# Fewer, larger loads in a delta-rule and gated-MLP kernel, and two kinds of transfer moved to ScalarE's queue

## The chip, the cores and the metric

The kernel runs on one core of a Trainium2 chip. A core has TensorE (PE: matrix products; its weight loads are listed as PEld), VectorE (DVE), ScalarE (ACT), GpSimd (POOL) and SyncE (SP, which only issues transfers and waits). The engines run side by side and meet at semaphores; each works through its own instructions strictly in order. Transfers (DMA) are carried by 16 DMA engines, whoever issues them. The metric is the device time of one execution in microseconds.

## The reference

The first half is a delta-rule attention, for each of 4 batches and 8 heads, with head size 48, over 768 steps in time. The second half is a gated MLP over its output.

```
k_n = k / (norm(k) + 1e-6)
for t in range(768):
    y[t]  = q[t] @ state                        # state: 48 x 48 for each head
    v_old = state^T @ k_n[t]
    state = state + beta[t] * outer(k_n[t], v[t] - v_old)

x = y, heads side by side                       # 4 x 768 x 384
h = relu(x @ w_in);  u, v = the two halves of h # 512 + 512 columns
v = (v - mean(v)) / sqrt(var(v) + 1e-6)
out = (u * (w_spatial @ v + b_spatial)) @ w_out # 4 x 768 x 384
```

All of it is float32. The MLP's products are made from two parts of each operand (`xh`, `xl`, `win_h`, `win_l` and so on), so that three products stand for one.

## The kernel before

**Chunks and steps.** The 768 time steps are cut into chunks of 64. One *step* of the kernel is one chunk of one batch with all eight heads (four pairs `u`, two halves `h` of the partitions): 48 steps, in two interleaved chains of two batches each. Within a chunk the recurrence becomes small matrix products with the inverse of a 64 x 64 triangular matrix per head.

**Groups and their inverses.** Four steps make a *group*; there are 12. For each step of a group `kk` loads K transposed (`k`, 112 partitions), multiplies it with itself on PE and masks and scales the result into `ta` on DVE (L595). When all four steps are there, `bounce` stores `ta` to DRAM (`ad`, two stores, L609) and `load_la` fetches the two 32 x 32 diagonal blocks of each matrix in another layout (`la`, four loads, L619): one block per partition, and each block twice, since two halves of the partitions work on the even and the odd columns of the same inverse. `lanes` copies a part of `la` into PSUM on ACT (L629, two copies), runs some 60 small substitution operations on DVE (L635 and L642), copies the result to `w` on ACT (L649), stores it to DRAM (`wd`, two stores, L655) and fetches it back into `ta` (four loads, L661). Group 0 goes another way (`lanes16`, `widen`) with 16 x 16 blocks.

**A step.** `load_kq` fetches K and Q transposed (`kq`, L680), `load_vk` fetches V and K in natural layout (`vk`, L684), each into one of three buffers; POOL scales V (L688). `step_t` transposes a part of the inverse (DVE, L703); `step_ef` completes the 64 x 64 inverse from its blocks (PE, with ACT's copies L717 and L729 between); `step_ab` takes the state's part off V (DVE L748) and multiplies with the inverse (DVE L764 writes `us`); `step_c` carries the state on (L792); `step_qk` and `step_d` make the output, which ACT writes to `xs` (L837). All small products of PE go through one helper, so they share line L412.

**The MLP.** When four chunks of a batch are done, `convert` packs them with six small transfers inside SBUF (L861), and ACT and POOL split `x` in its two parts (L868, L872). `mlp_v`, `mlp_u`, `mlp_g` and `mlp_o` (L903, L969, L1001, L1056) are the large products, which fill PE between the steps; ACT and DVE empty their PSUM tiles (among others L918, L980, L1018, L1037, L1065). The weights are loaded in pieces (`load_w`, L431 and L435) and split, mostly in the first third. L1239 are products with no use but to keep PE active.

**What sets the order.** The program is unrolled, and the order of the instructions on every engine is written by a planner in the kernel itself (`Line`). Every piece of work is a generator that yields an `Op`: its engine, how long it holds the engine (`occ`), when its result is there (`lat`), when it may begin (`dep`) and when it is due. The planner always takes the operation that can begin first by its own clock, and among those that are near, the one due first. What the operations really take on the chip is not known to it: an instruction whose input is late holds up everything behind it on its engine. A transfer costs SP 0.5 by this clock, and its data is taken to be there after `lat` (for a block load `la` 4.2):

```python
    return Op("SP", 0.5, lat, dep, due)
```

All transfers before are issued by SP. The bias, for comparison, is loaded in three pieces of one row that is repeated into two partitions (L1205):

```python
    out=x[32 * j : 32 * j + 2], in_=b_sp[j * 256 : j * 256 + 256].unsqueeze(0).broadcast_to([2, 256])
```

Of the kernel before, what the change touches and what calls it, by code (L numbers as in the profile page):

```python
# [7 lines left out]
F32 = mybir.dt.float32  # L8
# [11 lines left out]
G = 4  # L20
# [5 lines left out]
NG2 = NB * NT // 2  # L26
ND = DH // 128
KR = 112
EPS = 1e-6
LAG = 6  # L30
TG = 4
# [187 lines left out]
def dma(dep, due, lat=3.5, slack=0.0):  # L219
    if slack:  # L220
        first = dep

        def dep():
            t = first()
            return t if not t else t + slack

    return Op("SP", 0.5, lat, dep, due)


def now():  # L230
# [5 lines left out]
def delta_rule_gated_mlp(  # L236
    ctx: ExitStack,
    tc: tile.TileContext,
    kq_t: bass.AP,
    k_nat: bass.AP,  # L240
    vk_nat: bass.AP,
    b_nat: bass.AP,
    w_in: bass.AP,
    w_sp: bass.AP,
# [9 lines left out]
    def sb(name, *shape, dt=F32):  # L254
        return const.tile([128, *shape], dt, name=name)
# [72 lines left out]
    tmps = [sb(f"tmp{i}", 512) for i in range(2)]  # L328
    sms = [sb(f"sm{i}", 8) for i in range(4)]

    vks = [sb(f"vk{i}", 2 * NU * HD + 16) for i in range(3)]
    kqs = [const.tile([KR, 2, NU, CH], F32, name=f"kq{i}") for i in range(3)]
    kts = [const.tile([KR, NU, CH], F32, name=f"k{i}") for i in range(2)]
    aqs = [sb(f"aq{i}", NU, CH) for i in range(2)]
    mcs = [sb(f"mc{i}", NU, CH) for i in range(2)]
    tns = [sb(f"tn{i}", NU, 32) for i in range(2)]
# [45 lines left out]
    def on(t):  # L382
        return lambda: t

    def due(x):
        return lambda: x
# [7 lines left out]
    def rows_t(h):  # L394
        return slice(h * 64, h * 64 + 64)
# [27 lines left out]
        return Op("PE", 0, 1.3 * w, both(dep, slots[kind].ready), d, kind, make), held  # L423


    def load_w(buf, hi, lo, src, d):
        n = src.shape[1]
        st = buf[:, :n]
        if src.dtype == F32:
            t = yield dma(now, d, 6.0)  # L430
            nc.sync.dma_start(out=st, in_=src)  # L431
        else:
            raw = buf[:, 512 : 512 + 2 * n].bitcast(U32).rearrange("p (n two) -> p n two", two=2)
            t = yield dma(now, d, 6.0)
            nc.sync.dma_start(out=raw, in_=src.bitcast(U32).rearrange("p (n two) -> p n two", two=2))  # L435
            w0, w1 = raw[:, :, 0], raw[:, :, 1]
            e = buf[:, 256 : 256 + n].bitcast(U32)
            t1 = yield act(on(t), d, n)
            nc.scalar.activation(out=st, in_=w0, func=AF.Identity, scale=2.0**-52, bias=1.0)
            t = yield dve(on(t), d, n, 0.5)  # L440
            nc.vector.tensor_scalar(
                out=e, in0=w1, scalar1=20, scalar2=0x7FF, op0=ALU.logical_shift_right, op1=ALU.bitwise_and
            )
            t = yield dve(on(t), d, n, 0.5)
            nc.vector.tensor_scalar(out=e, in0=e, scalar1=896.0, scalar2=1150.0, op0=ALU.max, op1=ALU.min)
            t = yield dve(on(t), d, n, 0.5)
# [36 lines left out]
    def weights(par):  # L483
        buf = (*stage, ubs[3])[par]
        t = 0.0
        while jobs and (par < 2 or len(jobs) > n_late):
            hi, lo, src, kind = jobs.pop(0)
            t = yield from load_w(buf, hi, lo, src, due({"in": 3, "sp": 12, "out": 13}[kind]))
# [75 lines left out]
    def mask(t):  # L564
# [6 lines left out]
        )  # L571
        done["mc", t] = x

    def kk(t):
        g = t // G
        d = due(4 * g - 9)
        k = kts[t % 2] if t >= 2 * G else (
            xsb[t // 4][0:KR, t % 4 * 256 : t % 4 * 256 + 256].rearrange("p (u t) -> p u t", t=CH)
        )
        yield dma(at(("pk", t - 2) if t >= 2 * G + 2 else None), due(4 * g - 11), 3.5 if t < 2 * G else 6.0, 1.0)  # L580
        nc.sync.dma_start(out=k, in_=kq_t[t][:, 0])
        landed = line.t["SP"] + (3.0 if t < 2 * G else 5.5)
        free = [("b", s) for s in range((g - TG) * G, (g - TG) * G + G)] if g >= TG else []
        op, held = tiles_op(
            "anti",
            both(on(landed), at(("mc", t) if t >= G else None, *free)),
            d,
            lambda p: [mm(p[rows_t(h), u], k[rows_d(h), u, :], k[rows_d(h), u, :]) for u, h in UH],
            CH,
        )  # L590
# [4 lines left out]
        nc.vector.tensor_tensor(out=t_of(t), in0=psl(p[1], CH), in1=mcs[t % 2], op=ALU.mult)  # L595
        slots["anti"].give(p, x)
        done["kk", t] = x
# [5 lines left out]

    def bounce(g):
        d = due(4 * g - 7)
        ad = ad_g[g] = dram.tile([CH, 2, G * NU, CH], F32, name="ad")
        for h in range(2):
            t = yield dma(at(*(("kk", s) for s in range(g * G, g * G + G))), d, 4.5)
            nc.sync.dma_start(out=ad[:, h], in_=flat(g)[rows_t(h)])  # L609
        done["ad", g] = t  # L610

    def load_la(g):
        d = due(4 * g - 7)
        src = ad_g[g].rearrange("j h n t -> (h n) j t")
        for blk in range(2):
            for par in range(2):
                l0, r0 = par * 64 + blk * 32, blk * 32
                t = yield dma(at(("ad", g), ("lanes", g - 2) if g > 2 else None), d, 4.2)
                nc.sync.dma_start(out=las[g % 2][l0 : l0 + 32], in_=src[:, r0 : r0 + 32, r0 : r0 + 32])  # L619
        done["la", g] = t  # L620

    def lanes(g):
# [26 lines left out]
        nc.scalar.copy(out=ws, in_=w)  # L649
        done["wo", g] = t  # L650
        wd = dram.tile([32, 2, 2, G * NU, 32], F32, name="wd")
        wdl = wd.rearrange("c k h n t -> (k h n) c t")
        for par in range(2):
            t1 = yield dma(on(t), d, 4.5)
            nc.sync.dma_start(out=wdl[:, par::2, :], in_=ws[rows_t(par)])  # L655
        done["wd", g] = t1
        for blk in range(2):
            for h in range(2):
                r0 = h * 64 + blk * 32
                t = yield dma(on(t1), d, 4.0)  # L660
                nc.sync.dma_start(out=flat(g)[r0 : r0 + 32, :, blk * 32 : blk * 32 + 32], in_=wd[:, blk, h])  # L661
        done["T", g] = t


# [10 lines left out]
    def v_of(s):  # L675
        return vks[s % 3][:, 0 : NU * HD].rearrange("p (u e) -> p u e", e=HD)

    def load_kq(s):
        done["kq", s] = yield dma(at(*((n, s - 3) for n in ("qk", "d", "a") if s >= 3)), due(s - 2), 5.0, 1.0)
        nc.sync.dma_start(out=kqs[s % 3], in_=kq_t[s])  # L680

    def load_vk(s):
        t = yield dma(at(*((n, s - 3) for n in ("b", "c") if s >= 3)), due(s - 2.5), 5.0, 1.0)
        nc.sync.dma_start(out=vks[s % 3], in_=vk_nat[s])  # L684
        done["kn", s] = t
        v = v_of(s)
        x = yield pool(both(on(t), at(("cn", s // G))), due(s - 1.5), 192)
        nc.gpsimd.tensor_tensor(  # L688
            out=v, in0=v, in1=cns[s // G][:, s % G, 0].unsqueeze(2).broadcast_to([128, NU, HD]), op=ALU.mult
        )  # L690
        done["vs", s] = x
# [164 lines left out]
    def convert(j, xs, t):  # L856
        x = xs[1].rearrange("p (u t) -> p u t", t=256)
        for h in range(2):
            for i in range(NK):
                t1 = yield dma(on(t), lately(0.3), 2.4)  # L860
                nc.sync.dma_start(  # L861
                    out=x[h * 64 + 48 : h * 64 + 64, i],
                    in_=x[h * 64 + i * 16 : h * 64 + i * 16 + 16, 3],
                )
# [362 lines left out]
            line.spawn(lanes16())  # L1227

    def steps(s):
        for f in (load_kq, load_vk, step_t, step_ef, step_ab, step_c, step_qk, step_d):  # L1230
            line.spawn(f(s))
        if ORDER[s][2] == 0:
            line.spawn(zero(s))
# [104 lines left out]
```

## Time and profile before

| | |
|---|---|
| median of the runs | 597.86 us |
| the three runs | 594.10, 597.86, 601.64 us |
| the profiled execution | 594.68 us, its span 593.0 us |
| mean granted clock of TensorE | 0.902 |
| DMA, mean over the span | 64.31 MB, 108 GB/s |
| packets under 512 B, of all | 107,542 of 140,160 |

The span reaches from the first to the last instruction. Busy time is what an engine's own instructions cover; SP has none, and its issues are listed as SPq. The chain of waits starts from the last instruction and goes back, at each point, to what released it: its shares add up to the span, and they tell what ended last, which busy time doesn't. In a group's line the instructions are named by line, engine, operation and tiles (written<-read). A transfer's time to landing is counted from its issue to its semaphore.

Until 406 us, when the last inverses are loaded back (L661), steps, inverses and MLP share the engines; the last step's load is issued at 472 us (L680). What comes after is nearly all MLP.

### The profile page before, as it was taken

How to read it: one execution, taken by the hardware profiler on the slowest of the kernel's cores; microseconds unless marked ns; L12 is line 12 of the kernel's file. 1: busy time of each engine (PE TensorE's matmuls, PEld its weight loads, DVE VectorE, ACT ScalarE, POOL GpSimd, SP SyncE). 2: the span in 40 equal slices, each digit the busy share in tenths (PEclk: the TensorE clock that was granted, in tenths of full speed). 3: DMA queues.
4: the chain of work that ended last, by engine and by line, in shares of the span. 5: the costliest groups of instructions: out<-in, count | busy, mean ns of one | idle time of the engine just before them, and what ended most of it. 6: DMA issues, size and time to landing. Idle time of an engine off the chain costs nothing.

```text
span 593.0 us, 22265 instructions
## 1 busy us (share of the span) xinstructions
PE 521.4 (88%) x9404; PEld 474.3 (80%) x9404; DVE 352.9 (60%) x1436; ACT 216.8 (37%) x536; POOL 139.5 (24%) x210
## 2 busy tenths in 40 slices
PE   5935889889778997979999989999999999988997
PEld 5834868778657786979997878889988899977996
DVE  5799585977857988857995685871135422132220
ACT  3224334532334556223326456321256511155111
POOL 5452233652235242312204153120000000000000
PEclk9675586978878999979999899999999999997999
DMA  8767385676935766457736536333012200010001
GB/s 222 213 109 168 92 175 146 182 193 135 222 99 132 178 138 134 103 148 143 179 67 118 154 86 141 120 92 77 28 32 72 67 14 15 28 33 2 1 28 55
DMA packets 140160, 64.31 MB, mean 108 GB/s; under 512 B 107542, under 2 KB 130204, under 8 KB 140060
## 3 DMA queue, kind: packets, MB, share of 16 engines
q1 hardware_dynamic: 140060, 62.88, 43.7%
q8 instruction: 74, 1.21, 0.9%
q14 instruction: 26, 0.21, 0.1%
HBM read 47.55 MB, written 14.02 MB: 104 GB/s over the span
## 4 chain that ended last, share of the span: by engine, by line
PE 58%; DVE 18%; DMA 8%; SPq 6%; issue 5%; ACT 4%; POOL 1%; DVEq 0%; ACTq 0%; POOLq 0%
PE pt L412 21%; PE pm L1001 9%; PE pm L969 6%; PE pw L1001 6%; DVE prod L635 4%; DVE pw L642 4%; PE pm L1056 4%; PE pm L903 3%; PE pw L1056 3%; PE pw L903 2%; DMA kq<-in_kq_t 2%; PE pw L969 1%; SPq L861 1%; DVE ta L595 1%; SPq L619 1%
## 5 line engine op out<-in xcount | busy, mean ns | idle before, releaser
L642 DVE TENSOR_TENSOR pw<-pw,prod 128x30 f32<-128x30 f32 (+6 forms) x330 | 81.6, 251 | 5.4
L635 DVE TENSOR_TENSOR prod<-pw,la 128x30 f32<-128x30 f32 (+6 forms) x330 | 78.7, 241 | 6.9 <-ACT pw L629 1.7
L412 PE MATMUL pt<-kq,st 48*64 48x64 f32 x768 | 56.3, 239 | 2.1 <-ACT xs L837 1.7
L1001 PE MATMUL pm<-wsp_h,vh 128*128 128x256 f32 x192 | 57.4, 299 | 0.0
L412 PE MATMUL pt<-aq,us 64*64 64x64 f32 x768 | 54.4, 235 | 3.3 <-issue 3.0
L1001 PE MATMUL pm<-wsp_l,vh 128*128 128x256 f32 x192 | 54.7, 285 | 0.0
L1001 PE MATMUL pm<-wsp_h,vl 128*128 128x256 f32 x192 | 54.6, 284 | 0.0
L688 POOL TENSOR_TENSOR vk<-vk,cn 128x192 f32<-128x192 f32 x48 | 24.5, 512 | 116.7 <-DMA vk<-in_vk_nat 97.9
L412 PEld LDWEIGHTS pt<-aq,us 64*64 64x64 f32 x768 | 45.0, 149 | 3.5 <-issue 3.1
L412 PEld LDWEIGHTS pt<-kq,st 48*64 48x64 f32 x768 | 44.8, 148 | 3.6 <-ACT xs L837 1.8
L569 POOL TENSOR_TENSOR mc<-mpos,cn 128x256 f32<-128x256 f32 x46 | 28.9, 638 | 62.1 <-DVE cn L557 27.9
L412 PE MATMUL pt<-kq 48*64 48x64 f32 x768 | 37.9, 241 | 5.3 <-DMA kq<-in_kq_t 3.9
L412 PE MATMUL pt<-tn,ta 64*64 64x32 f32 x768 | 35.3, 237 | 7.3 <-DVE tn L703 3.8
L1239 PE MATMUL pm<-ones 128*128 128x256 f32 x216 | 39.5, 333 | 2.5 <-ACT ones L274 2.5
L1037 ACT CAST gh<-tmp 128x512 fp32r<-128x512 f32 x24 | 14.8, 619 | 70.3 <-DVE tmp L1018 70.2
L412 PE MATMUL pt<-us,vk 64*64 64x48 f32 x704 | 33.6, 235 | 7.5 <-DVE us L764 6.6
L412 PEld LDWEIGHTS pt<-tn,ta 64*64 64x64 f32 x768 | 30.8, 154 | 10.9 <-DVE tn L703 5.7
L412 PE MATMUL pt<-ta,pi 64*64 64x32 f32 x768 | 35.5, 235 | 3.8 <-ACT pi L717 2.0
L412 PE MATMUL pt<-k 48*64 48x64 f32 x640 | 30.4, 242 | 9.2 <-DMA k<-in_kq_t 6.8
L1001 PEld LDWEIGHTS pm<-wsp_h,vh 128*128 128x128 f32 x192 | 36.9, 192 | 1.5
L1018 DVE TENSOR_TENSOR tmp<-pm,ub 128x512 f32<-128x512 f32 x16 | 11.0, 688 | 45.4 <-PE pm L1004 45.4
L412 PEld LDWEIGHTS pt<-us,vk 64*64 64x64 f32 x704 | 28.1, 147 | 12.0 <-DVE us L764 8.8
(182 smaller groups left out, 1500.4 us busy)
## 6 DMA issues: line engine op xcount, KB each, us to landing
kq<-in_kq_t SPq DMA_DIRECT2D x48, 224.0 KB, 3.5
vk<-in_vk_nat SPq DMA_DIRECT2D x48, 200.0 KB, 3.4
ad<-ta SPq DMA_DIRECT2D x24, 256.0 KB, 4.2
la<-ad SPq DMA_DIRECT2D x44, 128.0 KB, 4.0
out<-ob SPq DMA_DIRECT2D x24, 192.0 KB, 1.9
k<-in_kq_t SPq DMA_DIRECT2D x40, 112.0 KB, 3.5
knn<-in_k_nat SPq DMA_DIRECT2D x10, 384.0 KB, 4.4
wd<-w SPq DMA_DIRECT2D x22, 128.0 KB, 3.6
```

What stands on the lines that cost most here:

```text
L412: return lambda: nc.tensor.matmul(*a, **dict(dict(start=True, stop=True), **k))
L569: (nc.vector if t in (0, 2) else nc.gpsimd).tensor_tensor(out=mc, in0=mall, in1=cns[t // G][:, t % G, 1].unsqueeze(2).broadcast_to([128, N ...
L635: nc.vector.tensor_tensor(out=pr, in0=w[:, :n, j : j + 1].broadcast_to([128, n, m]), in1=la[:, j, j + 1 : 32].unsqueeze(1).broadcast_to([1 ...
L642: nc.vector.tensor_add(out=w[:, :n, j + 1 : 32], in0=w[:, :n, j + 1 : 32], in1=pr)
L688: nc.gpsimd.tensor_tensor(out=v, in0=v, in1=cns[s // G][:, s % G, 0].unsqueeze(2).broadcast_to([128, NU, HD]), op=ALU.mult)
L903: nc.tensor.matmul(p[1], a[:, kt, ts], w[:, kt, DH:], start=(n == 0), stop=(n == 3 * NK - 1))
L969: nc.tensor.matmul(pu[:, k], w[:, kt, d0 : d0 + 128], a[:, kt], start=(n == 0), stop=(n == 3 * NK - 1))
L1001: nc.tensor.matmul(pg[:, k], v[:, d0 : d0 + 128], w[:, si, ts], start=(n == 0), stop=False)
L1018: nc.vector.tensor_tensor(out=gt, in0=pg, in1=ut[:, hs], op=ALU.mult)
L1037: nc.scalar.copy(out=gh[:, hs], in_=gt)
L1056: nc.tensor.matmul(p[1][:, :DM], a[:, dd, ts], w[:, dd], start=(n == 0), stop=(n == 3 * ND - 1))
L1239: nc.tensor.matmul(free[0].rearrange("p (n t) -> p n t", t=128), ones, ones.unsqueeze(1).broadcast_to([128, 2, 128]), start=True, stop=True,)
```

## The change

- **A step's loads.** `kq_t` and `vk_nat` become one input `kv_t`: for each step 128 rows of 912 numbers (K and Q transposed, then V and K natural, padded from 112 to 128 rows in the first part). `load_kq` and `load_vk` become `load_kv`, one load into one of three buffers, which waits for all readers of the buffer three steps back.
- **K of a group.** It comes by two steps with one load (all four steps of group 1 with one), from `kv_t`. From group 2 on there is one buffer of two steps instead of two buffers of one.
- **The bounce.** From group 1 on only the diagonal blocks are stored, by four stores (before: two stores of the whole matrices). They are then loaded by one load, whose source is repeated twice. The order of block and half in the lanes changes with it, in `wd` too.
- **Queues.** The six transfers that pack `x` and the two stores of the inverses are issued by ACT (`nc.scalar.dma_start`) instead of SP.
- **The planner.** A transfer costs SP 0.58 by its clock instead of 0.5, and ACT 0.6. Some latencies change (the block load 4.0 instead of 4.2, weights 4.5 instead of 6.0 with a slack of 1.5, K and step loads as in the diff); a K load's landing is now taken from the planned end of the load itself. A weight load becomes ready when its buffer's last piece is done, where before it was ready at once.

The core of the diff; the host's packing of `kv_t` is left out.

```diff
-    return Op("SP", 0.5, lat, dep, due)
+    return Op("SP", 0.58, lat, dep, due)
+
+
+def act_dma(dep, due, lat):
+    return Op("ACT", 0.6, lat, dep, due)
...
-    vks = [sb(f"vk{i}", 2 * NU * HD + 16) for i in range(3)]
-    kqs = [const.tile([KR, 2, NU, CH], F32, name=f"kq{i}") for i in range(3)]
-    kts = [const.tile([KR, NU, CH], F32, name=f"k{i}") for i in range(2)]
+    kvs = [sb(f"kv{i}", KV) for i in range(3)]
+    kqs = [x[0:KR, 0 : 2 * NU * CH].rearrange("p (a u t) -> p a u t", a=2, t=CH) for x in kvs]
+    vks = [x[:, 2 * NU * CH :] for x in kvs]
+    ktp = const.tile([KR, 2, NU, CH], F32, name="k")
...
-            t = yield dma(now, d, 6.0)
+            t = yield dma(on(t0), d, 4.5, 1.5)
...
-        k = kts[t % 2] if t >= 2 * G else (
-            xsb[t // 4][0:KR, t % 4 * 256 : t % 4 * 256 + 256].rearrange("p (u t) -> p u t", t=CH)
-        )
-        yield dma(at(("pk", t - 2) if t >= 2 * G + 2 else None), due(4 * g - 11), 3.5 if t < 2 * G else 6.0, 1.0)
-        nc.sync.dma_start(out=k, in_=kq_t[t][:, 0])
-        landed = line.t["SP"] + (3.0 if t < 2 * G else 5.5)
+        n = 2 if t < G or t >= 2 * G else G
+        if t % n == 0:
+            ks = ktp
+            if t < 2 * G:
+                ks = xsb[t // 4][0:KR, t % 4 * 256 : (t % 4 + n) * 256].rearrange("p (s u t) -> p s u t", s=n, t=CH)
+            kt_of[t // n, n] = ks
+            busy = [("pk", t - 1), ("pk", t - 2)] if t >= 2 * G + 2 else []
+            done["k", t] = yield dma(at(*busy), due(4 * g - 11), 4.0 if t < 2 * G else 5.0, 1.5)
+            nc.sync.dma_start(
+                out=ks.rearrange("p s u t -> p s (u t)"),
+                in_=kv_t[t : t + n, 0:KR, 0 : NU * CH].rearrange("s p c -> p s c"),
+            )
+        k = kt_of[t // n, n][:, t % n]
...
     def bounce(g):
         d = due(4 * g - 7)
+        if g:
+            ad = ad_g[g] = dram.tile([2, 2, G * NU, 32, 32], F32, name="ad")
+            for h in range(2):
+                for blk in range(2):
+                    r0, c0 = h * 64 + blk * 32, blk * 32
+                    t = yield dma(at(*(("kk", s) for s in range(g * G, g * G + G))), d, 4.0)
+                    nc.sync.dma_start(
+                        out=ad[h, blk].rearrange("n j t -> j n t"), in_=flat(g)[r0 : r0 + 32, :, c0 : c0 + 32]
+                    )
+            done["ad", g] = t
+            return
...
-        src = ad_g[g].rearrange("j h n t -> (h n) j t")
-        for blk in range(2):
-            for par in range(2):
-                l0, r0 = par * 64 + blk * 32, blk * 32
-                t = yield dma(at(("ad", g), ("lanes", g - 2) if g > 2 else None), d, 4.2)
-                nc.sync.dma_start(out=las[g % 2][l0 : l0 + 32], in_=src[:, r0 : r0 + 32, r0 : r0 + 32])
+        src = ad_g[g].rearrange("h k n j t -> (h k n) (j t)").unsqueeze(0).broadcast_to([2, 64, 1024])
+        t = yield dma(at(("ad", g), ("lanes", g - 2) if g > 2 else None), d, 4.0)
+        nc.sync.dma_start(out=las[g % 2].rearrange("p j t -> p (j t)"), in_=src)
...
-        wdl = wd.rearrange("c k h n t -> (k h n) c t")
+        wdl = wd.rearrange("c h k n t -> (h k n) c t")
         for par in range(2):
-            t1 = yield dma(on(t), d, 4.5)
-            nc.sync.dma_start(out=wdl[:, par::2, :], in_=ws[rows_t(par)])
+            t1 = yield act_dma(on(t), d, 4.5)
+            nc.scalar.dma_start(out=wdl[:, par::2, :], in_=ws[rows_t(par)])
...
-    def load_kq(s):
-        done["kq", s] = yield dma(at(*((n, s - 3) for n in ("qk", "d", "a") if s >= 3)), due(s - 2), 5.0, 1.0)
-        nc.sync.dma_start(out=kqs[s % 3], in_=kq_t[s])
-
-    def load_vk(s):
-        t = yield dma(at(*((n, s - 3) for n in ("b", "c") if s >= 3)), due(s - 2.5), 5.0, 1.0)
-        nc.sync.dma_start(out=vks[s % 3], in_=vk_nat[s])
-        done["kn", s] = t
+    def load_kv(s):
+        t = yield dma(
+            at(*((n, s - 3) for n in ("qk", "d", "a", "b", "c") if s >= 3)), due(s - 2.5), 4.5, 1.5
+        )
+        nc.sync.dma_start(out=kvs[s % 3], in_=kv_t[s])
+        done["kq", s] = done["kn", s] = t
...
-                t1 = yield dma(on(t), lately(0.3), 2.4)
-                nc.sync.dma_start(
+                t1 = yield act_dma(on(t), lately(0.3), 2.4)
+                nc.scalar.dma_start(
                     out=x[h * 64 + 48 : h * 64 + 64, i],
                     in_=x[h * 64 + i * 16 : h * 64 + i * 16 + 16, 3],
                 )
```

More of the change, by code (lines that the diff above doesn't have):

```diff
@@ L28 @@
 KR = 112
+KV = 2 * NU * CH + 2 * NU * HD + 16
 EPS = 1e-6
@@ L238, in delta_rule_gated_mlp @@
     tc: tile.TileContext,
-    kq_t: bass.AP,
+    kv_t: bass.AP,
     k_nat: bass.AP,
-    vk_nat: bass.AP,
     b_nat: bass.AP,
@@ L423, in tiles_op, with load_w @@
         return Op("PE", 0, 1.3 * w, both(dep, slots[kind].ready), d, kind, make), held
-    def load_w(buf, hi, lo, src, d):
+    def load_w(buf, hi, lo, src, d, t0):
         n = src.shape[1]
@@ L433, in load_w @@
             raw = buf[:, 512 : 512 + 2 * n].bitcast(U32).rearrange("p (n two) -> p n two", two=2)
-            t = yield dma(now, d, 6.0)
+            t = yield dma(on(t0), d, 4.5, 1.5)
             nc.sync.dma_start(out=raw, in_=src.bitcast(U32).rearrange("p (n two) -> p n two", two=2))
@@ L487, in weights @@
             hi, lo, src, kind = jobs.pop(0)
-            t = yield from load_w(buf, hi, lo, src, due({"in": 3, "sp": 12, "out": 13}[kind]))
+            t = yield from load_w(buf, hi, lo, src, due({"in": 3, "sp": 12, "out": 13}[kind]), t)
             left[kind] -= 1
@@ L572, in mask @@
         done["mc", t] = x
+    kt_of = {}
     def kk(t):
@@ L585, in kk @@
             "anti",
-            both(on(landed), at(("mc", t) if t >= G else None, *free)),
+            at(("k", t - t % n), ("mc", t) if t >= G else None, *free),
             d,
@@ L660, in lanes @@
                 t = yield dma(on(t1), d, 4.0)
-                nc.sync.dma_start(out=flat(g)[r0 : r0 + 32, :, blk * 32 : blk * 32 + 32], in_=wd[:, blk, h])
+                nc.sync.dma_start(out=flat(g)[r0 : r0 + 32, :, blk * 32 : blk * 32 + 32], in_=wd[:, h, blk])
         done["T", g] = t
@@ L1229, in steps @@
     def steps(s):
-        for f in (load_kq, load_vk, step_t, step_ef, step_ab, step_c, step_qk, step_d):
+        for f in (load_kv, step_t, step_ef, step_ab, step_c, step_qk, step_d):
             line.spawn(f(s))
@@ L1302 @@
     qt = dfirst(q)
-    kq_t = np.ascontiguousarray(np.stack([dfirst(k), qt], axis=2))
-    vk_nat = np.zeros((NST, 128, 2 * NU * HD + 16), k.dtype)
-    vk_nat[:, :, : NU * HD] = tfirst(v).reshape(NST, 128, NU * HD)
-    vk_nat[:, :, NU * HD : 2 * NU * HD] = np.roll(tfirst(k).reshape(NST, 128, NU * HD), 64, axis=1)
+    kv_t = np.zeros((NST, 128, KV), k.dtype)
+    kv_t[:, :KR, : NU * CH] = dfirst(k).reshape(NST, KR, NU * CH)
+    kv_t[:, :KR, NU * CH : 2 * NU * CH] = qt.reshape(NST, KR, NU * CH)
+    c0 = 2 * NU * CH
+    kv_t[:, :, c0 : c0 + NU * HD] = tfirst(v).reshape(NST, 128, NU * HD)
+    kv_t[:, :, c0 + NU * HD : c0 + 2 * NU * HD] = np.roll(tfirst(k).reshape(NST, 128, NU * HD), 64, axis=1)
     bt = beta.reshape(NB, NU, 2, NC_, CH).transpose(2, 4, 0, 3, 1).reshape(128, NST, NU)[:, perm_s]
@@ L1314 @@
     args_np = {
-        "kq_t": kq_t,
+        "kv_t": kv_t,
         "k_nat": tfirst(k),
-        "vk_nat": vk_nat,
         "b_nat": np.ascontiguousarray(bt),
```

## The prediction

> **What bounds the kernel now.** I read the page's busy shares first, then its chain of waits, the groups and sources of the issuing queue, and last the timeline where one load was late.
>
> ```profile
> PE 521.4 (88%) x9404; PEld 474.3 (80%) x9404; DVE 352.9 (60%) x1436; ACT 216.8 (37%) x536; POOL 139.5 (24%) x210
> PE 58%; DVE 18%; DMA 8%; SPq 6%; issue 5%; ACT 4%; POOL 1%; DVEq 0%; ACTq 0%; POOLq 0%
> PE pt L412 21%; PE pm L1001 9%; PE pm L969 6%; PE pw L1001 6%; DVE prod L635 4%; DVE pw L642 4%; PE pm L1056 4%; PE pm L903 3%; PE pw L1056 3%; PE pw L903 2%; DMA kq<-in_kq_t 2%; PE pw L969 1%; SPq L861 1%; DVE ta L595 1%; SPq L619 1%
> ```
>
> PE is busy for 88% of the span but holds only 58% of the chain; DVE's substitution in lanes (L635, L642) is next. What this change touches is the queue and the transfers: SPq 6% of 593.0 us is 36 us, DMA 8% is 47 us. No engine can gain more than that from them together, and only their removable part. The view of the sources gives the price of one issue (min/median/max in ns), and the view of transfers the time to landing (last column, us):
>
> ```profile
> L619 SPq DMA_DIRECT2D la<-ad x44: 303/564/2144, 29.0 to 368.2; - x44
> L609 SPq DMA_DIRECT2D ad<-ta x24: 466/492/761, 14.7 to 361.2; - x24
> L655 SPq DMA_DIRECT2D wd<-w x22: 597/660/1779, 75.6 to 400.4; - x22
> L861 SPq DMA_DIRECT2D xs<-xs x72: 512/586/1807, 88.1 to 533.4; - x72
> L581 SPq DMA_DIRECT2D k<-in_kq_t x40: 328/508/1639, 6.1 to 352.8; - x40
> L680 SPq DMA_DIRECT2D kq<-in_kq_t x48: 312/380/1723, 8.4 to 471.9; - x48
> ```
>
> ```profile
> kq<-in_kq_t SPq DMA_DIRECT2D x48, 224.0 KB, 3.5
> vk<-in_vk_nat SPq DMA_DIRECT2D x48, 200.0 KB, 3.4
> ad<-ta SPq DMA_DIRECT2D x24, 256.0 KB, 4.2
> la<-ad SPq DMA_DIRECT2D x44, 128.0 KB, 4.0
> knn<-in_k_nat SPq DMA_DIRECT2D x10, 384.0 KB, 4.4
> ta<-wd SPq DMA_DIRECT2D x44, 64.0 KB, 3.0
> xs<-xs SPq DMA_DIRECT2D x72, 16.0 KB, 1.8
> ub<-in_b_sp SPq DMA_DIRECT2D x3, 2.0 KB
> ```
>
> The last view is the one that sets my price for a late load: the chain, PE and ACT (idle time in brackets) around 156 us, where a kq load was late.
>
> ```profile
> 156.35 4.60 DMA kq<-in_kq_t
> ```
>
> ```profile
> 160.99 0.34 PE L412 MATMUL pt<-st,kq 48*64 48x48 f32 x1 [3.29 <-DMA kq<-in_kq_t]
> ```
>
> ```profile
> 162.21 0.27 ACT L729 COPY ta<-pt 128x128 f32<-128x128 f32 x1 [5.30 <-PE pt L412]
> 163.73 0.58 ACT L629 COPY pw<-la 64x512 f32<-64x512 f32 x1 [0.32 <-DMA la<-ad]
> 236.31 1.21 ACT L629 COPY pw<-la 64x512 f32<-64x512 f32 x2
> ```
>
> Of 4.60 us of lateness PE stood 3.29 us, a share of 0.72; ACT behind it stood 5.30. The order on every engine is fixed in advance, so whatever waits stops all that is queued behind it.
>
> **The change, part by part.** The sum is made against the profiled execution, 594.68 us with its span of 593.0; the median of the three runs shown, 597.86, is 3.2 higher, and they spread over 7.5.
>
> *One load per step.* kq and vk (48 + 48 issues) become 48 issues of 128 x 3,648 B, 456 KB. 48 x 0.380 = 18 us of SP issues go. Landing: knn's 384 KB takes 4.4 us, so some 5 against 3.5. It must wait for all five readers of step s-3; the kq load waits for the last of them (step_d) already, so v's scaling on POOL moves later by at most its wait for kq. Behind that load in SP's order are the K loads and the inverses, behind v's scaling L748 on DVE and the b product on PE. Ends: all of kq's 2% of the chain gone (-12 us) to 48 x 1.5 us later landing x 0.72 (+52). The load has step s-2 to land in, so I take -6.
>
> *K by two steps.* 48 issues become 23: 25 x 0.508 = 13 us of SP. From group 2 on there is one buffer of two steps, so a group's second pair waits for the first pair's products, and may come one landing later. Nine to ten such places x 4.4 us x 0.72 give at most +32; the products are due nine steps ahead of their group, which hides it: 0.
>
> *x and the inverses on ACT's queue.* 72 x 0.586 + 22 x 0.660 = 57 us of issues leave SP (SPq L861 has 1% of the chain, 6 us) and enter ACT's order. During 6 x 0.586 = 3.5 us per x tile ACT begins no copy of pi, ta or xs for the step in hand. If none is hidden that is 57 x 0.72 = +41; if all is, 0. ACT is at 37% and holds 4% of the chain, and the planner charges 0.6 each, so it can put urgent copies first: I take +5. SP's gain from this and from the four la issues that become one (33 x 0.564 = 19 us, SPq L619 another 1%) is 12 us, the two shares on the chain; ends -36 (all of SPq) to 0.
>
> *The bounce.* Two stores of 256 KB with 4 KB rows become four of 64 KB with 128 B rows in each group from 1 on: 22 more issues x 0.492 = 11 us of SP. The nearest row is ta<-wd, the same size and rows: 3.0 us, so 1.5 + 3.0 from the first issue against 0.5 + 4.2. That comes out even: 0, ends -2 to +1 us for each of 11 groups.
>
> *The group's blocks by one load.* This decides. Its destination is 128 rows of 4 KB, 512 KB; its source is written as a repeat of two in front of 64 rows (unsqueeze, broadcast to [2, 64, 1024]). Every large load of before has an outermost loop of 32 to 128 rows on both sides. The one transfer of the same form is the bias (L1205, a row repeated to [2, 256]): two packets of 1 KB, and the only row above without a landing time. It cannot tell whether a larger one is dealt by its 128 rows or by its repeat of two, so I bound it. The views of the transfers in two stretches (queue: packets, MB, share of 16 engines), and the busy share and GB/s of the first:
>
> ```profile
> q1 hardware_dynamic: 1245, 1.03, 89.3%
> ```
>
> ```profile
> 4.00:8.00 4.00, 4.00 (x140) 3.81 (x139) 3.01 (x8) 0.30 (x2) 3.58 (x12) 1.00 0.89 259
> ```
>
> ```profile
> q1 hardware_dynamic: 864, 1.18, 6.1%
> ```
>
> From 4 to 8 us (loads of 1 to 3 KB rows) one engine moved 1.03 MB / (16 x 4 x 0.893) = 18.0 GB/s; from 540 to 593 us (mostly output rows of 1.5 KB) 1.18 MB / (16 x 53 x 0.061) = 22.8 GB/s. Dealt over sixteen, 524 KB at 259 GB/s take 2.0 us, and with the 1.8 us that a 16 KB transfer takes to land, 3.8. Dealt over two, 262 KB each take 11.5 us (22.8) to 14.6 us (18.0), landing after 13.3 to 16.4. I take two engines, by the bias row, which alone has this form, and 13.3, since 4 KB rows are nearer to the longer ones.
>
> The Trainium skill, "DMA: Bandwidth & Descriptors", section "Why a DMA increments its semaphore by 16 and not by 1", states that a transfer is split along the outermost dimension that isn't 1, over the largest number of engines up to 16 that divides that dimension on both sides; its "Rules for kernel authors" name a leading repeat of c copies as confined to c engines. By that rule it would be two here, and at its 27 GiB/s per engine some 9 us of moving (an estimate from that page). No run here shows a broadcast load of this size yet; the bias row doesn't contradict it.
>
> Who waits: ACT's copy of la into PSUM (L629) stands in ACT's fixed order where the planner thinks that the load lands. Before, it began 6.3 us after the first la issue in group 5 and 9.3 in group 7:
>
> ```profile
> 157.43 3.60 SPq L619 DMA_DIRECT2D la<-ad  x4
> 227.03 3.29 SPq L619 DMA_DIRECT2D la<-ad  x4
> ```
>
> The planner charged three issues of 0.5 and 4.2, 5.7 us; it now charges 4.0, so the copy moves up by 1.7, to 4.6 and 7.6 after the issue, in the middle 6.1. ACT then stands 13.3 - 6.1 = 7.2 us, with pi, ta, xs and every MLP eviction behind it; DVE stands at the first L635 that reads that PSUM; and all of SP's later loads, the steps' among them, queue behind the blocks on those two engines. At 0.72 that is 5.2 us, and for 11 groups +57. Ends: none (sixteen engines) to 11 x (16.4 - 4.6) = +130.
>
> Sum: 594.7 - 6 - 12 + 5 + 57 = 639 for an execution like the profiled one; one like the median would be 3 higher. I take 640.
>
> **The rivals.** *Dealt over all sixteen (faster).* The load lands after 3.8 us, the planner's 4.0 is right, and three issues a group are saved: 594.7 - 13 = 582, or 571 if all of kq's share on the chain and another 5 us of SPq go. For it: 128 rows on the destination, as in every load that lands in 3 to 5 us. Against it: the source's form. The turning point is the landing: up to 6.1 us the copy doesn't wait, from about 7.5 us on (11 x 1.4 x 0.72 = 11) the saving is spent. *Late but covered (same).* The blocks do come after 13 us, but ACT's copy has fallen behind SP by then: the page of sources shows that copy waiting for its load in only three places, 1.6 us in all.
>
> ```profile
>   DMA la<-ad: 1.6, 3
> ```
>
> If the lead is 9 to 10 us, 11 x 3.5 x 0.72 = 28, or 18 with half of that under PE's MLP work: 594.7 - 13 + 18 = 600. Against it: with fewer issues SP is no later than before, and the copy's due time was moved up. *ACT's queue becomes the wait (slower by another way).* Blocks over sixteen, but the 94 issues on ACT cost their +41: 594.7 - 18 + 41 = 618. Against it: 4% of the chain. That an edit does nothing at all is excluded: the counts of issues are in the code.
>
> **How the numbers follow.** Forecast (two engines, the copy waits) 0.68; sixteen engines 0.16; late but covered 0.12; ACT's issues 0.04. The forecast's own range is 610 (594.7 - 13 + 28: cover of PE's MLP work halves the 57) to 690 (594.7 - 13 + 11 x 7.2 = 79, every microsecond passed on, a third as much again for the loads behind the blocks, and 3 for the median), and holds nine in ten of its 0.68. With the covered case, ACT's and the upper third of the faster case the range is 582 to 690. Two per cent, 12 us, is about what a measurement of this kernel can tell from no change. Faster by over 2% is the sixteen-engine case, 0.16; within 2% the covered one with the forecast's lowest edge, 0.14; slower 0.70.
>
> **What would show it.** Right: the block load's time to landing is 11 us or more (it may have no landing time, like the bias), ACT L629 heads the list of waits with about 7 us in each of 11 places, PE's idle time rises at those places, and SPq L861 is gone from the chain. If ACT L629 waits for nothing and the load lands in 4 us, the sixteen-engine rival holds. If L629 is prompt and ACT's L717 or L729 stand behind issues, it is ACT's queue. If PE waits for kv at many steps without a block load in front, the price of the merged load was mine to get wrong.

## The result and the profile after

The changed kernel takes 685.74 us (median of 4 runs, 677.30 to 685.81) against 599.25 us for the kernel before (median of 4 runs beside it): a ratio of 1.142, 95% interval 1.130 to 1.154. It is slower, as forecast, but the slowdown of 86 us is twice the forecast one of 42. The profiled execution took 685.81 us with a span of 684.1. Here and below, some executions of a kernel run at a lower granted clock and come out over 1.5% longer than its fastest: the ratios leave these out and compare the means of the others, while the medians count all executions, so that the two can differ by about 1%.

The page's busy shares, and below them its chain of waits. The chain's shares add up to only about half of the span: on the way back from the end it was lost, so they tell of the later half.

```profile
PE 543.0 (79%) x9500; PEld 496.1 (73%) x9500; DVE 357.1 (52%) x1436; ACT 217.4 (32%) x536; POOL 139.4 (20%) x210
PE 29%; DMA 9%; DVE 5%; ACT 3%; issue 2%; ACTq 2%; SPq 1%; DVEq 0%
PE pt L417 7%; PE pm L1021 6%; DMA la<-ad 4%; PE pw L1021 3%; PE pm L1076 3%; PE pw L1076 2%; PE pm L989 2%; DMA out<-ob 2%; PE pm L923 2%; ACTq L881 1%; PE pw L923 1%; DVE pw L664 1%; DVE prod L657 1%; DMA ta<-wd 1%; DMA ad<-ta 1%
```

No engine has more to do: DVE is at 357.1 us of work against 352.9, ACT at 217.4 against 216.8. PE's 22 us more come with a lower granted clock (0.837 over the span against 0.902). What grew most is idle time: 141 us of the span on PE, against 72 before. The block load la<-ad, which had no share worth a line before, now heads the transfers of the chain, and with it stand the output's store, the inverses' return (ta<-wd) and the blocks' stores. The view of the waits (us in total, times, longest) says who stands for them:

```profile
ACT pw L651 <- DMA la<-ad: 64.8, 8, 10.6
DVE prod L657 <- ACT pw L651: 30.7, 6, 7.7
ACT ob L1085 <- DMA out<-ob: 26.2, 7, 10.7
PE pt L417 <- DMA k<-in_kv_t: 19.4, 1, 19.4
PE pt L417 <- DMA kv<-in_kv_t: 10.8, 4, 3.9
```

ACT's copy of the blocks (L651, before L629) waits in 8 of the 11 groups for 8.1 us each; before it was 1.6 us in all. That is the wait that the prediction named. The third and fourth rows are of another kind: an output store and a K load have nothing to do with the blocks, and they are waited for longer than before (17.1 us and 6.8 us there). One place shows how they come together, in the timelines of SP and ACT:

```profile
388.92 0.55 SPq L641 DMA_DIRECT2D la<-ad  x1
389.57 14.04 SPq L1088 DMA_DIRECT2D out<-ob  x2
```

```profile
391.27 0.83 ACT L888 CAST xh<-xs 128x768 fp32r<-128x768 f32 x1 [0.59 <-PE pm L923]
402.75 0.48 ACT L1085 COPY ob<-pm 128x384 f32<-128x384 f32 x1 [10.65 <-DMA out<-ob]
```

SP issues the block load at 388.92 and right behind it, at 389.57, the store of a finished output tile. Stores of this kind landed after 1.9 us before; this one frees its buffer only 13 us later, and ACT stands 10.65 us for it. The chain and the windows of the stretch (busy time of PE, PEld, DVE, ACT, POOL, then the granted clock, the share of the 16 DMA engines and GB/s) show what happened in between:

```profile
389.57 13.16 DMA out<-ob
461.68 13.99 DMA la<-ad
```

```profile
395.00:400.00 5.00, 0.00 (x0) 0.00 (x0) 0.00 (x0) 0.00 (x0) 0.00 (x0) 0.66 0.13 52
```

For five microseconds no engine of the core does anything. The DMA engines are busy to a share of 0.13, which is 2 of 16, and move 52 GB/s, 26 each. This row is the direct sight of the two engines. It fits the 13.16 us of the output store that every other transfer behind the blocks has its own share on these two as well, and isn't complete until they have got to it. That holds for ACT's queue too: its two stores of the inverses were issued at 389.24 and 390.07 us, and of the packets moved from 395 to 400 us 62 are SP's (0.25 MB, the blocks) and 62 ACT's (0.01 MB); from 400 to 402 us it is 28 of each. Equal counts of such unequal packets say that the two queues took turns on the busy engines, one short row of the stores for one 4 KB row of the blocks.

The stop has an after-effect: the granted clock is 1.00 until 395 us, 0.66 in the row above, 0.50 from 400 to 405 and 0.55 to 407, and then 1.00 again. So the products right behind a stop run slower, which is a part of PE's 22 us more; how large a part was not summed up.

### The profile page after: what moved, and what is told of

Its sections match the earlier page's. It is cut to its first block, busy times and chain, and to the rows that moved or that the text cites. A ratio compares the mean times of both kernels' runs of the same rounds, so it can differ in the third digit from the quotient of the medians.

```text
span 684.1 us, 22247 instructions
## 1 busy us (share of the span) xinstructions
PE 543.0 (79%) x9500; PEld 496.1 (73%) x9500; DVE 357.1 (52%) x1436; ACT 217.4 (32%) x536; POOL 139.4 (20%) x210
## 4 chain that ended last, share of the span: by engine, by line
PE 29%; DMA 9%; DVE 5%; ACT 3%; issue 2%; ACTq 2%; SPq 1%; DVEq 0%
PE pt L417 7%; PE pm L1021 6%; DMA la<-ad 4%; PE pw L1021 3%; PE pm L1076 3%; PE pw L1076 2%; PE pm L989 2%; DMA out<-ob 2%; PE pm L923 2%; ACTq L881 1%; PE pw L923 1%; DVE pw L664 1%; DVE prod L657 1%; DMA ta<-wd 1%; DMA ad<-ta 1%
## 5 line engine op out<-in xcount | busy, mean ns | idle before, releaser
L657 DVE TENSOR_TENSOR prod<-pw,la 128x96 f32<-128x96 f32 (+10 forms) x330 | 77.9, 241 | 35.3 <-ACT pw L651 30.7
L664 DVE TENSOR_TENSOR pw<-pw,prod 128x96 f32<-128x96 f32 (+11 forms) x330 | 80.7, 250 | 4.4
L417 PE MATMUL pt<-kv,st 48*64 48x64 f32 x768 | 63.6, 256 | 0.9 <-DVE us L784 0.6
L417 PEld LDWEIGHTS pt<-ta,pi 64*64 64x64 f32 x768 | 36.5, 174 | 24.2 <-ACT pi L737 22.1
L417 PE MATMUL pt<-kv,ta 64*64 64x48 f32 x768 | 41.1, 252 | 16.2 <-ACT ub L1000 8.1
L417 PEld LDWEIGHTS pt<-kv,st 48*64 48x64 f32 x768 | 50.2, 165 | 3.2 <-issue 1.4
L417 PE MATMUL pt<-kv 48*64 48x64 f32 x768 | 39.3, 248 | 14.9 <-DMA kv<-in_kv_t 10.8
L417 PEld LDWEIGHTS pt<-kv,ta 64*64 64x64 f32 x768 | 35.0, 163 | 21.5 <-ACT ub L1000 8.3
L1259 PEld LDWEIGHTS pm<-ones 128*128 128x128 f32 x213 | 37.3, 252 | 14.8 <-ACT ob L1085 9.8
L417 PEld LDWEIGHTS pt<-kv 48*64 48x64 f32 x768 | 32.2, 156 | 17.9 <-DMA kv<-in_kv_t 8.4
```

The source lines that it names most:

```text
L417: return lambda: nc.tensor.matmul(*a, **dict(dict(start=True, stop=True), **k))
L657: nc.vector.tensor_tensor(out=pr, in0=w[:, :n, j : j + 1].broadcast_to([128, n, m]), in1=la[:, j, j + 1 : 32].unsqueeze(1).broadcast_to([1 ...
L664: nc.vector.tensor_add(out=w[:, :n, j + 1 : 32], in0=w[:, :n, j + 1 : 32], in1=pr)
L1259: nc.tensor.matmul(free[0].rearrange("p (n t) -> p n t", t=128), ones, ones.unsqueeze(1).broadcast_to([128, 2, 128]), start=True, stop=True,)
```

## The experiments

Ratios are to the kernel before, run on the same chip beside each kernel, with their 95% interval; medians are in us. Chips differ by up to 6 us in the kernel before (593 to 599), so ratios are what is compared.

**The repeat taken away.** The block load becomes two loads of 64 rows.

```diff
-        src = ad_g[g].rearrange("h k n j t -> (h k n) (j t)").unsqueeze(0).broadcast_to([2, 64, 1024])
-        t = yield dma(at(("ad", g), ("lanes", g - 2) if g > 2 else None), d, 4.0)
-        nc.sync.dma_start(out=las[g % 2].rearrange("p j t -> p (j t)"), in_=src)
+        src = ad_g[g].rearrange("h k n j t -> (h k n) (j t)")
+        for par in range(2):
+            t = yield dma(at(("ad", g), ("lanes", g - 2) if g > 2 else None), d, 4.0)
+            nc.sync.dma_start(out=las[g % 2][rows_t(par)].rearrange("p j t -> p (j t)"), in_=src)
```

> The changed kernel, with the one block load of a group issued as two loads of 64 rows without the repeat, 256 KB each, so that each has an outermost loop of 64 on both sides. Theory A (the repeat confines the load to two engines, and what waits for it makes the whole slowdown): the loads land after 3 to 5 us instead of 14, ACT's copy waits under 5 us in all instead of 64.8, and the time falls to 575 to 595 us. Rival B (the issues on ACT's queue, and SP's wait for the stores made there): the block load is only a bystander, the time stays above 640. Rival C (the merged step load is the wait): also above 640, with PE's waits for kv unchanged.

Measured: 604.91, ratio 1.011 (1.005 to 1.018). The source view of the copy, with the rows of its waits:

```profile
L652 ACT COPY pw<-la x22: 576/584/586, 38.5 to 390.5; 64x512 f32<-64x512 f32 x22
  issue: 1.6, 1
  DMA la<-ad: 0.7, 1
```

The copy's wait fell from 64.8 to 0.7 us and 0.13 of the 0.142 went with it. The loads land after 6.3 us (median), later than the 3 to 5 expected, and the time lies above what theory A expected: 10 us by the median, 6 if the ratio is taken on the 594 us of the kernel before. The blocks are nearly the whole slowdown, but what is left isn't faster than before either.

**The planner told of the slow load.** One number, `d, 4.0` to `d, 14.0`, in the changed kernel's block load.

> The changed kernel with one number changed: the planner is told that the block load takes 14.0 instead of 4.0. The load itself stays as it is, on two engines. Theory A1 (most of the cost is that ACT's copy stands in the order ten microseconds too early): the copy waits under 15 us in all, and the time falls by about 11 x 5 = 55 us, to 610 to 640. Theory A2 (most of the cost is that every later load queues behind the blocks on those two engines, and that the inverses come ten microseconds later): under 20 us are won, the time stays at 665 to 690.

Measured: 645.49, ratio 1.091 (1.081 to 1.102), between the two theories: by the ratios 0.051 of the kernel before is won, some 30 us, and 0.091, some 54 us, is still lost. In its source view the copy waits for nothing any more, but PE and ACT wait for other transfers (view of the waits):

```profile
PE pt L417 <- DMA kv<-in_kv_t: 23.4, 5, 7.3
PE pt L417 <- DMA k<-in_kv_t: 22.2, 3, 19.6
ACT ob L1085 <- DMA out<-ob: 22.0, 8, 6.2
POOL kv L708 <- DMA kv<-in_kv_t: 126.1, 21, 29.9
```

**The blocks' part alone on the kernel before.** The four stores, the repeated load, and the order of `wd` that goes with them; `load_kq`, `load_vk`, K, queues and the other numbers as before.

> The kernel before with the blocks' part of the change alone: four stores of the diagonal blocks and the one repeated load (planner's latency 4.0), all on SP, step loads, K loads, queues and the other planner costs as before. Theory A: it has nearly the whole slowdown, 660 to 690 us. Rivals B and C: without their parts it stays under 620.

Measured: 674.83, ratio 1.141 (1.132 to 1.150): the whole slowdown comes with this part.

**The queues put back.** The kernel with two block loads, and

```diff
-            t1 = yield act_dma(on(t), d, 4.5)
-            nc.scalar.dma_start(out=wdl[:, par::2, :], in_=ws[rows_t(par)])
+            t1 = yield dma(on(t), d, 4.5)
+            nc.sync.dma_start(out=wdl[:, par::2, :], in_=ws[rows_t(par)])
```

and the same for the packing of x.

> As the run with two loads of 64 rows, and the packing of x and the stores of the inverses put back to SP's queue. Theory A: the queues matter little, within 2% (12 us) of the run with two loads. Rival B: faster than that run by more than 12 us, and SP's wait for the stores of the inverses (37.7 us in the changed kernel) goes.

Measured: 595.16, ratio 1.004 (0.999 to 1.009). By the medians that is 10 us under the run with ACT's queue, by the ratios 4, and their intervals overlap; either way it is within the 12 us of theory A. The block loads land after 4.2 us here, against 6.3 there. SP's wait for the stores of the inverses is mostly gone, as rival B expected; in the run with ACT's queue and in this one:

```profile
SPq L684 <- DMA wd<-w: 31.9, 11, 5.9
```

```profile
SPq L684 <- DMA wd<-w: 8.7, 5, 3.5
```

With the stores on ACT, SP arrives at their return trip before they have landed in 11 places instead of 5, and everything behind it in SP's order waits. What this costs in time isn't clear of the noise.

**Two loads, and the planner told 14.0 all the same** (both `d, 4.0` to `d, 14.0`).

> The run with two block loads (604.9 us), with the planner told that each takes 14.0 although it takes some 4: the inverses come as late in the fixed order as in the run where the planner was told of the slow load (645.5 us), but no engine is held by the blocks. If the 40 us between those two runs come from the inverses standing ten microseconds later in the order, this run takes 635 to 650 us. If they come from the later loads that queue behind the blocks on two engines, it takes 600 to 615 us.

Measured: 617.72, ratio 1.036 (1.026 to 1.045), nearer to the second expectation and just outside it. Against the run with two loads in their early place (1.011) the late place costs 0.025 here; against the run told 14.0 (1.091), where the load holds two engines, 0.055 is won, some 33 us. The order isn't quite the same in these runs, since two loads are one issue more for each group.

**The blocks' part alone, with two loads.** The third experiment with the edit of the first.

> The kernel before with the blocks' part alone (as the run with 674.8 us), the block load issued as two loads of 64 rows without the repeat. Theory A: the whole of that run's slowdown goes, 585 to 600 us. If the four stores with 128 B rows were to blame for a part of it: 610 us or more. It also shows what this part would have been worth without the repeat: with 22 issues less for the loads and 22 more for the stores I expect no difference to the kernel before beyond 1%.

Measured: 587.19, ratio 0.988 (0.982 to 0.993). The four stores with their short rows cost nothing that shows; without the repeat this part alone gains a little more than 1%, where I had expected no more than that. Its transfers (KB each, us to landing):

```profile
la<-ad SPq DMA_DIRECT2D x22, 256.0 KB, 3.9
ad<-ta SPq DMA_DIRECT2D x44, 64.0 KB, 2.8
```

**The queues alone, and the merged step load alone, on the kernel before.** The first is the edit of the diff in `lanes` and `convert` with `act_dma`; the second has `kv_t`, `load_kv` and its three buffers, with K still loaded step by step, from `kv_t`.

> The kernel before with the packing of x and the stores of the inverses on ACT's queue (planner's cost 0.6 on ACT), nothing else changed. The difference between the two runs with two block loads (604.9 with ACT's queue, 595.2 without) says 600 to 608 us, 1 to 2% slower than before. If ACT's queue only hurts beside the merged loads and K pairs: 590 to 597 us.

> The kernel before with the step's two loads merged to one, K loads, blocks, queues and the other planner costs as before. The prediction put this part at -6 us: 585 to 590 us. If the issues it saves were not what ended last, within 1% of the kernel before; if the later landing counts, 600 us or more.

Measured: 593.49, ratio 0.989 (0.982 to 0.996) for the queues, the second branch: alone, ACT's queue doesn't hurt. That it hurts beside the other parts isn't shown, since 1.011 and 1.004 there have intervals that overlap. 591.08, ratio 0.990 (0.982 to 0.998) for the merged load: the median is just above the first range, and by the ratio it is 6 us under the kernel before, which is what the prediction gave it, with an interval of 1 to 11 us.

**The slow load issued by ACT.** In the run told 14.0:

```diff
-        t = yield dma(at(("ad", g), ("lanes", g - 2) if g > 2 else None), d, 14.0)
-        nc.sync.dma_start(out=las[g % 2].rearrange("p j t -> p (j t)"), in_=src)
+        t = yield act_dma(at(("ad", g), ("lanes", g - 2) if g > 2 else None), d, 14.0)
+        nc.scalar.dma_start(out=las[g % 2].rearrange("p j t -> p (j t)"), in_=src)
```

> The run where the planner was told 14.0 (645.5 us), with the repeated block load issued from ACT's queue instead of SP's; it still moves on two engines. If the 28 us between the late run with two loads (617.7) and that run come from SP's later loads standing in one line behind the blocks, they now stand in another line and most of it goes: 615 to 630 us. If they come from the two engines being busy, whoever asks, it stays at 638 to 655 us; ACT's wait for the stores of the blocks may add some.

Measured: 647.06, ratio 1.090 (1.084 to 1.097), the same as from SP. The queue that asks doesn't matter to the time, but it does to the waits: PE's for the steps' loads fall from 23.4 us to 5.8, those for K from 22.2 to 17.5, ACT's for the output's store from 22.0 to 15.6. Other idle time takes their place; whether it is ACT's own wait for the blocks' stores was not separated.

**Three parts together, and two parts alone.** The blocks with two loads, the merged load and ACT's queue, with K and the planner's numbers as before; then K by two steps alone (`kt_of`, one buffer of two); then the planner's numbers alone (`Op("SP", 0.58, ...)`, and `load_w` with `on(t0)`, 4.5 and 1.5).

> The kernel before with the merged step load, ACT's queue for x and the inverses, and the blocks' part with two loads of 64 rows, but with K step by step and the planner's other numbers as before. Each of the three alone measured 0.988 to 0.990 of the kernel before. If they add up: 0.965 to 0.975, about 577 us. If each only shortens the same line of SP: 0.985 to 0.995.

> The kernel before with K of a group by two steps (one buffer of two) alone. The run with two block loads and all the rest of the change stands at 1.011, though three of its parts alone are at 0.99. If the K pairs give that back: 1.01 to 1.03. The prediction put them at 0: 0.99 to 1.005.

> The kernel before with the planner's other numbers of the change alone: SP 0.58 for a transfer, weights 4.5 with a slack of 1.5 and ready only when the buffer's last piece is done. If the new order of the instructions gives the gain back: 1.01 to 1.03; if not, 0.99 to 1.005, and the K pairs remain.

Measured: 596.10, ratio 1.004 (0.999 to 1.008) for the three together, though each alone is at 0.988 to 0.990, above both expectations; 593.04, ratio 0.998 (0.994 to 1.002) for the K pairs, 0 as predicted; 584.59, ratio 0.987 (0.982 to 0.991) for the numbers alone, under both expectations, a gain where I had asked for a loss.

**The bytes alone.** The changed kernel, and the run told 14.0, with the same order of all instructions and a block load of a sixteenth:

```diff
+    for x in las:
+        nc.vector.memset(x.rearrange("p j t -> p (j t)"), 0.0)
...
-        src = ad_g[g].rearrange("h k n j t -> (h k n) (j t)").unsqueeze(0).broadcast_to([2, 64, 1024])
+        src = ad_g[g].rearrange("h k n j t -> (h k n) (j t)")[:, 0:64].unsqueeze(0).broadcast_to([2, 64, 64])
...
-        nc.sync.dma_start(out=las[g % 2].rearrange("p j t -> p (j t)"), in_=src)
+        nc.sync.dma_start(out=las[g % 2].rearrange("p j t -> p (j t)")[:, 0:64], in_=src)
```

> The changed kernel with the block load cut to the first two of each block's 32 rows (64 of 1,024 numbers per partition, 256 B; the rest of the buffer is zero, so most of the substitution works on zeros and the output isn't the reference's). Form, queue, count and the order of every instruction stay those of the changed kernel; only the bytes on the two engines fall to a sixteenth, and the landing to about 3 us. If the load's duration is the whole of what the blocks cost, as much is won as by two loads (604.9 us): 595 to 610. If the form costs something besides its duration, 620 or more.

> The same cut load in the run where the planner was told 14.0 (645.5 us): again the same order, with a load of about 3 us. If the 28 us that the slow load costs there beyond the late order come from the time for which the blocks hold two engines, they go: 610 to 625 us, like the late run with two loads (617.7). If they come from the different order that one issue gives: it stays at 638 to 650.

Measured: 597.61, ratio 1.008 (1.005 to 1.012), the first expectation, and 593.62, ratio 0.999 (0.995 to 1.003), even below its expectation. This pair is the cleanest cut. With the order held, the load's duration costs 0.134 of the kernel before where the copy stands early, and 0.092, some 55 us, where the copy waits for nothing.

The late order itself costs nothing in this pair (0.999 against 1.008), but 0.025 in the pair with two loads (1.036 against 1.011). Either the one issue more for each group makes another order there, or the zeros help here; no run decides it. So what the slow load costs beyond the copy's wait lies between 0.055 and 0.092, 33 to 55 us. The waits of the run told 14.0 with the small load, beside those shown above for the full one:

```profile
PE pt L419 <- DMA k<-in_kv_t: 9.0, 1, 9.0
PE pt L419 <- DMA kv<-in_kv_t: 5.3, 2, 4.1
ACT ob L1087 <- DMA out<-ob: 15.4, 6, 5.1
POOL kv L710 <- DMA kv<-in_kv_t: 81.0, 20, 30.3
```

PE's waits for the steps' and K's loads fall from 45.6 to 14.3 us, without a change in when they are issued in the order. They were held behind the blocks. That the substitution works mostly on zeros here doesn't change the instructions. In the early place the granted clock is no higher with them either (0.910, against 0.925 with two loads and the real numbers, in the profiled executions); in the late place it is (0.922 against 0.883), and whether the zeros have a part in that was not tested.

**The two best parts together**: the blocks with two loads and the planner's numbers.

> The kernel before with the two parts that gained most alone: the blocks' part as two loads (0.9875) and the planner's numbers for SP and the weights (0.9866). If the two gains are of different kinds they add to 0.972 to 0.98. If each is what a new order of instructions happens to give, the sum may lie anywhere from 0.98 to 1.01, as with the three parts that measured 1.0036 together.

Measured: 584.21, ratio 0.988 (0.981 to 0.995): no more than either alone. By the ratios, these three are the fastest kernels of this study, 1.2 to 1.3% under the kernel before.

## Why the prediction was half right

*Two engines: right.* The choice rested on the form that the load shares with the bias row; the row itself could not tell the number of engines, as the prediction says. The share of 0.13 in the silent stretch shows two, and two loads without the repeat land after 3.9 to 6.3 us, by run. The rule in the Trainium skill's "DMA: Bandwidth & Descriptors", "Why a DMA increments its semaphore by 16 and not by 1", holds here: with two copies outermost, two engines, with 64 rows outermost, no such limit. The estimate of 9 us of moving, by that page's rate for one engine, is near the 262 KB / 26 GB/s = 10.1 us of this trace. The same page's advice, in "Rules for kernel authors", against two transfers for two halves of the partitions, is given for halves that both run over all 16 engines. It doesn't carry over to a choice between them and a repeated source: here the two are 0.13 of the kernel faster than the one.

*Landing after 13.3 us: right in size.* 13.99 us from issue to copy in the last group, with a faster rate than the 22.8 GB/s that I took and more than 1.8 us around it.

*The copy's wait: right in size; how much of it was passed on stays open.* Forecast 7.2 us in each of 11 groups, measured 8.1 in 8 of them, 64.8 us against 79. When the copy was put where the load lands, 0.051 of the kernel before came back, some 30 us, not 57: 0.47 of the wait, not 0.72, if the late order costs nothing by itself. If it costs the 0.025 of the pair with two loads, the wait was worth 0.076, some 45 us or 0.70 of it. That this is near 0.72 would be luck: the 4.60 us behind that share are a load's time from issue to landing, of which PE stood 3.29, and not a wait of which a part reaches the end.

*The term that failed* is in the sentence "all of SP's later loads, the steps' among them, queue behind the blocks on those two engines". It named the mechanism and gave it no price in the sum; only the upper end of the forecast's own range had it, as a third of the copy's wait. It measured 0.055 to 0.092, about 33 to 55 us or 3 to 5 us for each block load; the smaller price goes with 45 us for the copy's wait, the larger with 30. It isn't covered by that wait: where the copy waits for nothing it is still there, because K and the output's store have their own waiters (22.2 and 22.0 us, against 9.0 and 15.4 with the small load), and the three buffers of a step's load did not hide its lateness (PE's 23.4 us against 5.3). The sum has no term for the lower clock behind a stop either; its share in these figures was not measured.

*The saving of 13 us did not come.* Without the slow load the rest of the change stands at 1.008 to 1.011, 5 to 7 us slower than before, not 13 faster. Part by part, by the ratios on some 595 us, no term fell short: the merged load -6 (forecast -6), K by pairs -1 (forecast 0), the queues -7 and the blocks with two loads -7 (forecast -12 + 5 for the two), and the planner's numbers -8, for which the forecast had no term. What fell is the addition. Three parts at 0.99 give 1.004 together, two at 0.987 give 0.988. The run with the queues put back points at one cause, SP's wait for stores that ACT now issues, but its 4 us are not clear of the noise; the rest is open. It fits that every edit of a cost or a length gives the planner another order, worth about a per cent either way, but this was not tested by itself. The shares of SPq on the chain were no measure of what removing issues brings; that PE's and DVE's work behind them takes over would explain it, but isn't shown.

*The rivals.* Sixteen engines: excluded by the share of 0.13. Late but covered: excluded by the 64.8 us (its sum has a slip: half of 28 is 14 and not 18, so that it would have stood at 596 instead of 600). ACT's queue as the wait: some 4 us beside the merged loads, within the noise, near the 5 that I took and far from its 41.

## What to carry to other kernels

Before merging loads, look at the outermost loop on both sides of the transfer: a repeat of two in front turned sixteen engines into two, and cost more than all the issues it saved. Price a slow transfer twice, once for its own reader and once for everything that is issued behind it while it holds its engines; the second was 33 to 55 us here, beside 45 to 30 for the first. And a share of the chain is an upper end for what an edit can save: where the order is planned anew with each edit, add gains only after measuring them together.

## What the runs showed of the hardware

Transfers that run over all engines are held up by one that fills two of them, whether it comes from the same queue or from the other. From the same: a store of 192 KB that lands in 1.9 us otherwise took 13 us behind a 512 KB load on two engines, while from 393 to 403 us the sixteen were busy to a share of only 0.13 to 0.16. From the other: the packets of ACT's stores of the inverses went one for one with the blocks' from 395 to 402 us, and were still moving at 402. In time the queue made no difference (1.091 with the slow load from SP, 1.090 from ACT). The Trainium skill states, in "DMA: Bandwidth & Descriptors", "Issuing engines are not separate DMA queues", that transfers from different engines run on the same 16 and interleave; the 62 packets of each queue agree, and so does the run from ACT's queue, in that it gained nothing.
